# Planning the instruction order of a fused recurrence and MLP anew, with loads modelled as landing later

## The chip, the cores and the metric

The kernel runs on one core of one Trainium2 chip. The metric is the device time of one execution in microseconds (us), the median over several runs. The engines of a core are TensorE (PE in the profile, with its weight loads as PEld), VectorE (DVE), ScalarE (ACT), GpSimd (POOL) and SyncE (SP), which issues the DMA transfers. Each works through its own queue of instructions in order, and waits where an instruction's inputs are not there.

## The reference

A complex diagonal recurrence runs over 768 positions of 32 heads with 48 channels. Its output goes through an MLP with a softplus between two matrices (384 to 2,048 to 384).

```python
def _attn_ref(q, k, v, a_re, a_im):
    B, H, S, D = q.shape                       # 4, 8, 768, 48
    mag = np.sqrt(a_re * a_re + a_im * a_im)
    scale = np.minimum(mag, 0.999) / (mag + 1e-06)
    a_re_n, a_im_n = (a_re * scale, a_im * scale)
    ...
    for t in range(S):
        ar, ai = (a_re_n[:, :, t, :, None], a_im_n[:, :, t, :, None])
        new_re = ar * S_re - ai * S_im
        new_im = ar * S_im + ai * S_re
        kv = np.einsum('bhd,bhe->bhde', k[:, :, t], v[:, :, t])
        S_re, S_im = (new_re + kv, new_im)
        y[:, :, t] = np.einsum('bhd,bhde->bhe', q[:, :, t], S_re)

def _moe_ref(x, w_in, w_out):
    h = x @ w_in                               # 3072 x 384 @ 384 x 2048
    g = np.maximum(h, 0.0) + np.log1p(np.exp(-np.abs(h)))
    return g @ w_out                           # 3072 x 2048 @ 2048 x 384
```

## The kernel before

**Tiles and stages.** The recurrence is cut into chunks of 128 positions. There are 24 chunks: chunk `gc` is position block `gc // 4` of batch `gc % 4`. Four chunks, one block of all batches, make a group of 512 tokens, which is the unit of the MLP. Fourteen slices (0 to 3 with one chunk each, 4 to 13 with two) go through `pre`: ScalarE and VectorE turn `a_re` and `a_im` (the loads of lines 447 and 449, tiles `x_0` to `x_3`, then `x01_4`, `x23_4` and so on) into decays and phases. Line 471 ends the logarithm of the magnitude (tile t1), line 497 sums it along the positions on TensorE for the first four slices (`sum`; a scan at line 480 for the later ones), line 521 is the arctangent, lines 524 to 526 are the sines, and lines 544 and 546 multiply q and k by them. The sines and the arctangent need another ScalarE table than the logarithms and exponentials; line 827 is the place of a table load.

`chunk` then does one chunk. SyncE copies q and k into another layout (`qk`, line 581, ten DMA issues) and loads `v` (line 454). TensorE transposes k (`tr`, line 604), ScalarE copies it (`kt`, lines 609 to 612), TensorE makes the state update (`kv`, line 682), the scores (`sc`, line 627) and the output (`y`, lines 658 and 661); VectorE masks the scores (`a`, line 630). Lines 669 to 671 split y into a high and a low part, `xt0` and `xt1`.

`moe` does the MLP of a group in steps of 128 of the 2,048 hidden channels: nine matmuls for `h` (line 717), three ScalarE passes (lines 722 to 724) and VectorE work (725 to 729) for the softplus and its split into `gh` and `gl`, nine matmuls into the three accumulators `o` (line 741). There are 96 such steps; below, h25 means the 25th h in TensorE's order.

The weights come as eight blocks each of `w_in` and `w_out` (`raw_wi`, `raw_wo`, line 339). They are 64-bit words: VectorE takes their bits apart (349, 352, 355), ScalarE or VectorE rounds (362 or 364), VectorE keeps the rest (366), and `wi0`, `wo0` and so on are ready. Beside this, `inspect` loads all weights once more in 32 pieces (`seen0` to `seen31`, line 384, 384 KB each), and two ScalarE passes (391 and 392) check their size.

**What sets the order.** No queue is written by hand. All of the above are tasks for a `Planner`, each with an engine, a modelled duration, its buffers and a key. `order` plays the program through once, when the kernel is built: at each modelled instant every free engine takes the ready task with the smallest key, and the order in which tasks were taken is the order of the instructions. Keys come from the table `K`: where a slice begins (`head`, `turn`, `tail`), where each chunk, state update, weight block and MLP group stands, how far loads are ahead (`rlead`, `xlead`, `vlead`, `plead`), from where the inspected weights are due (`seen`, and `seenstep` from one to the next), and a few penalties. Some copies and casts may go to ScalarE or VectorE, whichever the model finds free (`alt`). For a DMA the model has one line of transfer: it starts 0.65 us after the issue or when the transfer ahead is done, moves at a fixed rate, and its data are ready a fixed time after. An issue is held back while more than `backlog` us of transfers are outstanding.

When the model finds nothing ready for TensorE, after the first `sum` and before the first `o`, it puts in a filler: one 128x128 matmul whose result nobody reads (line 777), modelled at 0.214 us, so that the array does not stand still. Fillers are ordinary instructions: they are run also if the data are there earlier than modelled.

Of the kernel before, what the change touches and what calls it, by code (L numbers as in the profile page):

```python
# [84 lines left out]
class Planner:  # L85
# [48 lines left out]
    def order(self, filler, until, gate):  # L134
        for t in self.tasks:
            t.left = len(t.deps)
            t.ready = 0.0
            for d in t.deps:
                d.outs.append(t)
        engines = ("PE", "ACT", "DVE", "POOL", "SP")  # L140
        free = dict.fromkeys(engines, 0.0)
        pend = {e: [] for e in engines}
        alts = {"POOL": [], "ACT": [], "DVE": []}
        for t in self.tasks:
            if not t.left:
                pend[t.eng].append(t)
        live, users, queue, slots = {}, {}, {}, {}
        first = {}
        for t in reversed(self.tasks):
            t.key = min([t.key] + [o.key for o in t.outs])  # L150
        for t in self.tasks:
            for b in t.bufs:
                first.setdefault(b, (t.key, t.idx))
        for b in sorted(first, key=lambda b: first[b]):
            queue.setdefault(b.tag, []).append(b)
            live[b.tag] = set()
            slots[b.tag] = list(range(b.bufs))

        def room(t):
            need = {}  # L160
            for b in t.bufs:
                if b not in live[b.tag]:
                    need.setdefault(b.tag, []).append(b)
            for tag, bs in need.items():
                if len(live[tag]) + len(bs) > bs[0].bufs or not all(b in queue[tag][: len(bs)] for b in bs):
                    return False
            return True

        ends, freed = [], []
        dma_free = 0.0  # L170
        table = "log"
        out = []
        now = 0.0
        done = 0
        n = len(self.tasks)
        while done < n:
            for x in [x for x in ends if x[0] <= now]:
                ends.remove(x)
                t = x[1]
                done += 1  # L180
                for b in t.bufs:
                    users[b] = users.get(b, b.users) - 1
                    if users[b] == 0:
                        freed.append((t.end + self.FREE, b))
                for o in t.outs:
                    o.left -= 1
                    o.ready = max(o.ready, t.end + self.LAT[t.eng][o.eng])
                    if not o.left:
                        pend[o.eng].append(o)
                        for a in o.alt:  # L190
                            alts[a].append(o)
            for x in [x for x in freed if x[0] <= now]:
                freed.remove(x)
                live[x[1].tag].discard(x[1])
                slots[x[1].tag].append(x[1].slot)
            nxt = min((x[0] for x in ends + freed), default=None)
            for e in engines:
                if free[e] > now:
                    nxt = free[e] if nxt is None else min(nxt, free[e])
                    continue  # L200
                best = None
                for t in pend[e] + (alts[e] if e in alts else []):
                    if t.ready > now:
                        nxt = t.ready if nxt is None else min(nxt, t.ready)
                        continue
                    if not room(t):
                        continue
                    if e == "SP" and dma_free > now + K["backlog"]:
                        nxt = dma_free - K["backlog"] if nxt is None else min(nxt, dma_free - K["backlog"])
                        continue  # L210
                    if t.eng != e:
                        work = max(0.0, free[t.eng] - now) + sum(
                            u.dur for u in pend[t.eng] if u.ready <= now and (u.key, u.idx) < (t.key, t.idx))
                        if work + t.dur < t.alt[e][0] + K["altpen"]:
                            continue
                    k = t.key + (K["tpen"] if t.tab and t.tab != table else 0.0)
                    if best is None or (k, t.idx) < best[0]:
                        best = ((k, t.idx), t)
                if best is None and e == "PE" and ends and gate.end and not until.end:
                    t = Task("PE", 0.214, filler, 0, -1, None, 0)  # L220
                    free[e] = now + self.array(now, t.dur)
                    t.end = free[e]
                    out.append(t)
                    nxt = min(nxt, free[e]) if nxt is not None else free[e]
                if best is None:
                    continue
                t = best[1]
                pend[t.eng].remove(t)
                if t.eng != e:
                    t.dur, t.fn = t.alt[e]  # L230
                    t.eng = e
                for a in t.alt:
                    if t in alts[a]:
                        alts[a].remove(t)
                for b in t.bufs:
                    if b not in live[b.tag]:
                        live[b.tag].add(b)
                        queue[b.tag].remove(b)
                        b.slot = slots[b.tag].pop(0)
                dur = t.dur  # L240
                if t.tab and t.tab != table:
                    dur += K["table"]
                    table = t.tab
                if e == "PE":
                    dur = self.array(now, dur)
                free[e] = now + dur
                t.end = now + dur
                if e == "SP":
                    dma_free = max(dma_free, now + dur + 0.65) + t.nbytes / 360e3
                    t.end = dma_free + 0.9  # L250
                ends.append((t.end, t))
                out.append(t)
                nxt = min(nxt, free[e]) if nxt is not None else free[e]
            if done < n:
                assert nxt is not None and (nxt > now or any(x[0] <= now for x in ends)), [(e, [(t.key, t.idx, [b.name for b in t.bufs]) for t in pend[e]][:6]) for e in engines]
                now = max(now, nxt)
        self.span = now
        return out
# [18 lines left out]
class Prog:  # L277
# [651 lines left out]
    def tokens(self):  # L929
# [72 lines left out]

K = {
    "head": [
        147.46, 624.17, -734.94, 397.74, -65.21, 161.81, 154.84, 126.74, 332.35, 200.17, 1147.56, 464.07,
        422.42, 1751.28,
    ],
    "turn": [
        875.87, 931.1, 671.81, 372.5, 881.48, 209.67, 360.72, 269.87, 526.4, 568.29, 228.13, 811.71, 706.01,
        1996.71,  # L1010
    ],
    "tail": [
        -334.95, 866.41, -128.28, 1028.77, 17.61, 491.11, 317.86, 1067.36, 517.27, 187.54, 259.83, 490.08,
        795.91, 848.69,
    ],
    "chunk": [
        -267.74, -147.68, 202.11, 211.6, 177.5, 1433.56, 639.03, 1244.43, 174.52, 599.91, 1309.15, 2182.89,
        343.73, 939.25, 322.68, 1047.42, 1525.38, 564.81, 348.78, 1828.49, 378.39, 329.92, 407.62, 379.87,
    ],
    "state": [  # L1020
        -1424.69, -194.39, -93.44, -28.82, 43.46, 43.95, 100.96, 52.68, 129.28, 129.32, 145.62, 150.03,
        185.36, 156.97, 189.71, 254.96, 277.69, 291.22, 297.54, 306.48, 1107.79, 715.4, 146.67, 173.29,
    ],
    "wgt": [
        96.27, -203.72, -101.3, 339.5, -596.58, 402.72, -145.78, 1172.96, 397.64, 873.73, 429.78, 354.94,
        258.65, 1931.67, 500.63, 58.25,
    ],
    "moe": [
        39.42, 84.93, 163.49, 185.18, 356.83, 370.86, 421.4,
    ],  # L1030
    "step": [
        2.126, 3.53, 0.332, 5.405, 0.484, 6.552, 40.863,
    ],
    "seen": 130.1,
    "seenstep": 19.706,
    "rlead": 77.677,
    "xlead": -372.318,
    "vlead": -60.991,
    "plead": -498.518,
    "backlog": 1.925,  # L1040
    "altpen": -0.18,
    "tpen": 9.371,
    "table": 1.3,
}

# [64 lines left out]
```

## Time and profile before

| what | us |
|---|---|
| median of 3 runs | 617.56 |
| lowest and highest of them | 616.93, 620.88 |
| the profiled execution, its own time | 621.91 |
| its span, first to last instruction | 620.2 |
| TensorE busy | 591.4 |
| ScalarE busy | 441.8 |
| VectorE busy | 437.6 |

All rows that are quoted below come from that one profiled execution. A row of the order of time gives start and length in us, engine, line, operation, result and inputs, shapes, the number of instructions merged (x), and in brackets the idle time of the engine just before it with the instruction or DMA that ended it. A row of a group gives busy time and the mean length in ns, then the idle time before its members. Lengths of TensorE rows overlap, since matmuls are pipelined: what a row takes is the distance to the start of the next. ScalarE, VectorE and TensorE are all busy most of the time, so the question at each place is which of them the others wait for.

### The profile page before, as it was taken

The numbers are of one execution on the slowest core, as the hardware profiler recorded it, in microseconds if no ns is written. First come the engines' busy times: TensorE is split into PE (matmuls) and PEld (weight loads), VectorE is DVE, ScalarE is ACT, GpSimd is POOL, SyncE is SP. The second block draws the span as 40 slices with busy tenths as digits, with TensorE's granted clock in tenths as the row PEclk, the third lists the DMA queues.
The fourth block names the chain that finished last, engine by engine and source line by source line (L and its number), as shares of the span: only waits on it lengthen the run. The fifth ranks groups of instructions, "written<-read, shape, count | busy, mean of one in ns | idle before, by whom it ended". The sixth has DMA issues, their size and how long they took to land.

```text
span 620.2 us, 11238 instructions
## 1 busy us (share of the span) xinstructions
PE 591.4 (95%) x4388; PEld 497.0 (80%) x4388; DVE 437.6 (71%) x653; ACT 441.8 (71%) x813; POOL 1.8 (0%) x16
## 2 busy tenths in 40 slices
PE   1999999999999998999999999999999989999995
PEld 1999998787878886878788888888788868888883
DVE  4698989989989886667784559777757624433532
ACT  7958596958997784956974696877949645568652
POOL 1000000000000000000000000000000000000000
PEclk9999999999999997999999999999999989999998
DMA  8948845244004354255340337135324420018002
GB/s 328 382 136 262 308 155 166 59 127 142 26 1 108 128 149 147 66 144 177 99 112 1 130 84 217 43 85 208 82 61 143 112 93 2 1 47 284 1 1 56
DMA packets 50940, 75.53 MB, mean 122 GB/s; under 512 B 5824, under 2 KB 42176, under 8 KB 50880
## 3 DMA queue, kind: packets, MB, share of 16 engines
q1 hardware_dynamic: 50880, 74.73, 38.8%
q8 instruction: 37, 0.61, 0.4%
q14 instruction: 23, 0.19, 0.1%
HBM read 50.33 MB, written 5.51 MB: 90 GB/s over the span
## 4 chain that ended last, share of the span: by engine, by line
PE 60%; ACT 14%; DVE 13%; DMA 7%; SPq 3%; issue 2%; DVEq 0%; ACTq 0%
PE o L741 21%; PE h L717 21%; PE sc L627 5%; PE o L777 4%; PE kv L682 3%; DMA x<-dense_dram 3%; ACT L827 2%; SPq L581 2%; DVE lt L725 2%; DMA seen<-w_out_dram 2%; PE y L661 2%; ACT lt L722 1%; PE y L658 1%; DVE t L480 1%; ACT lt L724 1%
## 5 line engine op out<-in xcount | busy, mean ns | idle before, releaser
L717 PE MATMUL h<-xt,wi 128*128 128x512 f32 x864 | 222.9, 403 | 4.7 <-DVE lt L725 2.5
L741 PE MATMUL o<-gh,wo 128*128 128x512 f32 x576 | 197.7, 400 | 0.4 <-ACT gh L728 0.4
L717 PEld LDWEIGHTS h<-xt,wi 128*128 128x128 f32 x864 | 161.9, 191 | 43.7 <-DVE lt L725 3.9
L725 DVE SCALAR_TENSOR_TENSOR lt<-h,lt 128x512 f32<-128x512 f32 x96 | 65.9, 688 | 104.2 <-ACT lt L724 104.1
L741 PEld LDWEIGHTS o<-gh,wo 128*128 128x128 f32 x576 | 108.4, 188 | 26.8 <-issue 1.6
L722 ACT ACTIVATE lt<-h 128x512 f32<-128x512 f32 x96 | 57.0, 594 | 85.9 <-PE h L717 83.6
L741 PE MATMUL o<-gl,wo 128*128 128x512 f32 x288 | 113.9, 396 | 0.7 <-DVE gl L729 0.7
L724 ACT ACTIVATE lt<-lt,one 128x512 f32<-128x512 f32 x96 | 69.5, 724 | 2.1
L729 DVE TENSOR_TENSOR gl<-lt,gh 128x512 fp32r<-128x512 f32 x96 | 66.0, 688 | 6.8 <-ACT gh L728 5.2
L741 PEld LDWEIGHTS o<-gl,wo 128*128 128x128 f32 x288 | 54.3, 188 | 13.6 <-DVE gl L729 2.1
L723 ACT ACTIVATE lt<-lt 128x512 f32<-128x512 f32 x96 | 60.6, 631 | 2.1
L627 PE MATMUL sc<-qk 96*128 96x128 f32 x384 | 49.7, 283 | 0.0
L627 PEld LDWEIGHTS sc<-qk 96*128 96x128 f32 x384 | 47.7, 198 | 1.5 <-issue 0.2
L777 PE MATMUL o<-ident 128*128 128x128 f32 x378 | 46.8, 279 | 0.0
L777 PEld LDWEIGHTS o<-ident 128*128 128x128 f32 x378 | 44.7, 195 | 0.6 <-issue 0.6
L480 DVE TENSOR_TENSOR_SCAN t<-hold,t 128x384 f32<-128x384 bf16 x40 | 36.1, 945 | 4.2 <-DMA out_dram<-o 3.3
L827 ACT ACT_TABLE_LOAD x28 | 35.9, 1283 | 0.5
L544 DVE TENSOR_TENSOR x<-x,t 128x1536 f32<-128x1536 f32 (+1 forms) x14 | 21.4, 1527 | 19.1 <-ACT t L526 19.1
L630 DVE TENSOR_TENSOR a<-sc,mask 128x512 f32<-128x512 f32 x48 | 32.3, 683 | 3.2 <-PE sc L627 3.2
L682 PEld LDWEIGHTS kv<-v,kt 128*96 128x96 f32 x320 | 29.8, 166 | 5.1 <-ACT kt L609 3.7
L391 ACT ACTIVATE seen<-seen 128x384 f32<-128x384 f32 x32 | 17.4, 547 | 22.2 <-DMA seen<-w_out_dram 18.0
L682 PE MATMUL kv<-v,kt 128*96 128x64 f32 (+1 forms) x320 | 29.9, 247 | 2.8 <-ACT kt L609 2.8
(90 smaller groups left out, 629.0 us busy)
## 6 DMA issues: line engine op xcount, KB each, us to landing
x<-dense_dram SPq DMA_DIRECT2D x20, 768.0 KB, 5.8
qk<-x SPq DMA_DIRECT2D x96, 144.0 KB, 3.3
raw_wi<-w_in_dram SPq DMA_DIRECT2D x8, 768.0 KB, 10.5
raw_wo<-w_out_dram SPq DMA_DIRECT2D x8, 768.0 KB, 10.1
seen<-w_in_dram SPq DMA_DIRECT2D x16, 384.0 KB, 3.8
seen<-w_out_dram SPq DMA_DIRECT2D x16, 384.0 KB, 3.9
v<-vpad_dram SPq DMA_DIRECT2D x24, 224.0 KB, 2.7
out_dram<-o SPq DMA_DIRECT2D x18, 256.0 KB, 3.2
```

What stands on the lines that cost most here:

```text
L480: V.tensor_tensor_scan(out()[:, s], self.hold, inc()[:, s], 0.0, ALU.mult, ALU.add)
L627: PE.matmul(psc()[:, hh * P : (hh + 1) * P], q[:, h, CH:], q[:, h, :CH], start=True, stop=True)
L682: PE.matmul(kv()[: 2 * D, s], k[:, h, :, :].rearrange("p c d -> p (c d)"), v[:, s], start=h == 0, stop=h == H - 1)
L717: PE.matmul(h()[:, :n], w()[:, q, i, fs], x()[:, i, :n], start=k == 0, stop=k == 3 * NI - 1)
L722: add("ACT", a1(n) - 0.04, lambda: A.activation(tv(), h(), AF.Abs), k, r=[h], w=[t])
L723: add("ACT", a1(n), lambda: A.activation(tv(), tv(), AF.Exp, scale=-1.0), k, w=[t], tab="log")
L724: add("ACT", a1(n, 1), lambda: A.activation(tv(), tv(), AF.Ln, bias=self.one), k, w=[t], tab="log")
L725: add("DVE", d1(n), lambda: V.scalar_tensor_tensor(tv(), h(), 0.0, tv(), ALU.max, ALU.add), k, r=[h], w=[t])
L729: add("DVE", d1(n), lambda: V.tensor_tensor(gl(), tv(), gh().bitcast(F32), ALU.subtract), k, r=[t, gh], w=[gl])
L741: PE.matmul(acc[m]()[:, :n], w()[:, wq, f % 2, ms], x(), start=f == f0 and q == 0, stop=f == f1 - 1 and q == 2)
L777: self.nc.tensor.matmul(self.acc0[0]()[:, :P], self.ident, x, start=True, stop=True)
L827: nc.scalar.preload_act_table_set(TABLES[table])
```

## The change

The model of a DMA gets a lower rate (330 GB/s for 360) and a later landing (2.0 us after the transfer for 0.9). Nothing else in the code differs but the table `K`, all of whose keys are other numbers; a few rows of it are shown.

```diff
                 if e == "SP":
-                    dma_free = max(dma_free, now + dur + 0.65) + t.nbytes / 360e3
-                    t.end = dma_free + 0.9
+                    dma_free = max(dma_free, now + dur + 0.65) + t.nbytes / 330e3
+                    t.end = dma_free + 2.0
...
     "wgt": [
-        96.27, -203.72, -101.3, 339.5, -596.58, 402.72, -145.78, 1172.96, 397.64, 873.73, 429.78, 354.94,
-        258.65, 1931.67, 500.63, 58.25,
+        447.27, -1169.33, -352.53, 1086.75, -1104.67, 201.72, -638.13, 1996.3, 1081.53, 701.56, 725.41,
+        1796.95, 1182.85, 1292.24, 1033.56, 59.41,
     ],
...
-    "seen": 130.1,
-    "seenstep": 19.706,
...
-    "backlog": 1.925,
...
+    "seen": 222.447,
+    "seenstep": 23.851,
...
+    "backlog": 3.992,
```

The work is the same, task for task; what moves is the order, which engine does some of the copies and casts, and the number of fillers. Before, 182 fillers stand ahead of the first h and 7 behind it; now 155 and 1. Three places follow, as the instruction queues have them (the number behind a tile's name tells buffers apart).

TensorE, from the second half of chunk 3's scores to the first h, before:

```order
L627 MATMUL sc3_1_747<-qk3_631 128x128 x4
L777 MATMUL o0_153<-ident_58 128x128 x12
L661 MATMUL y3_774<-a3_0_762,v3_546 32x128 x6
L661 MATMUL y3_774<-a3_1_767,v3_546 32x128 x6
L661 MATMUL y3_774<-a3_0_762,v3_546 32x128 x2
L661 MATMUL y3_774<-a3_1_767,v3_546 32x128 x2
L777 MATMUL o0_153<-ident_58 128x128 x32
L717 MATMUL h_849<-xt0_0_434,wi0_838 128x512
```

and now:

```order
L627 MATMUL sc3_1_730<-qk3_594 128x128 x4
L777 MATMUL o0_162<-ident_58 128x128 x20
L661 MATMUL y3_773<-a3_0_752,v3_556 32x128 x6
L661 MATMUL y3_773<-a3_1_762,v3_556 32x128 x6
L661 MATMUL y3_773<-a3_0_752,v3_556 32x128 x2
L661 MATMUL y3_773<-a3_1_762,v3_556 32x128 x2
L777 MATMUL o0_162<-ident_58 128x128 x16
L717 MATMUL h_822<-xt0_0_470,wi0_809 128x512
```

The 32 fillers behind y3 became 16, and the 12 ahead of it 20.

VectorE in the first twenty microseconds, from the end of slice 0's logarithm (t_0, line 471) on, before:

```order
L471 SCALAR_TENSOR_TENSOR t_0_104<-t_0_104,x_0_97 128x384
L471 SCALAR_TENSOR_TENSOR t_1_114<-t_1_114,x_1_100 128x384
L504 COPY car00_157<-sum0_0_144 128x3
L460 TENSOR_TENSOR x_3_106<-x_3_106,t_3_148 128x384
L461 TENSOR_TENSOR t_3_148<-x_3_106,t_3_148 128x384
L462 SCALAR_TENSOR_TENSOR t_3_148<-t_3_148,x_3_106 128x384
L504 COPY car00_157<-sum0_1_164 128x3
L534 TENSOR_SCALAR t_0_104<-sum1_0_178 128x384
```

and now:

```order
L471 SCALAR_TENSOR_TENSOR t_0_108<-t_0_108,x_0_97 128x384
L349 TENSOR_SCALAR bits_wo0_146<-raw_wo0_106 128x768
L352 SCALAR_TENSOR_TENSOR bits_wo0_146<-raw_wo0_106,bits_wo0_146 128x768
L460 TENSOR_TENSOR x_3_103<-x_3_103,t_3_133 128x384
L471 SCALAR_TENSOR_TENSOR t_1_113<-t_1_113,x_1_99 128x384
L461 TENSOR_TENSOR t_3_133<-x_3_103,t_3_133 128x384
L355 SCALAR_TENSOR_TENSOR bits_wo0_146<-raw_wo0_106,bits_wo0_146 128x768
L462 SCALAR_TENSOR_TENSOR t_3_133<-t_3_133,x_3_103 128x384
L364 CAST wo0_178<-bits_wo0_146 128x768
L349 TENSOR_SCALAR bits_wi2_185<-raw_wi2_111 128x768
L366 TENSOR_TENSOR wo0_178<-bits_wo0_146,wo0_178 128x768
L534 TENSOR_SCALAR t_0_108<-sum1_0_180 128x384
```

The conversion of wo0, and the start of wi2's, now stand between the steps of slices 1 and 3; before, the first conversion came after line 544 of slices 0 and 1. SyncE's queue has `raw_wo0` as the sixth load now and as the ninth before. Its first four are the first halves of x_0 to x_3 now; before, x_0's second half stood second.

ScalarE around the copies of chunk 11's transposed k (kt11), before:

```order
L724 ACTIVATE lt_2423<-lt_2423,one_66 128x512
L391 ACTIVATE seen2_2385<-seen2_2385 128x384
L670 ACTIVATE xt0_2_2231<-y10_2389 128x3x128
L609 ACTIVATE kt11_2450<-tr11_0_2430 128x6x48
L611 ACTIVATE kt11_2450<-tr11_0_2430 128x2x32
L612 ACTIVATE kt11_2450<-tr11_0_2430 128x2x16
```

and now:

```order
L722 ACTIVATE lt_2203<-h_2181 128x512
L609 ACTIVATE kt11_2215<-tr11_0_2198 128x6x48
L611 ACTIVATE kt11_2215<-tr11_0_2198 128x2x32
L612 ACTIVATE kt11_2215<-tr11_0_2198 128x2x16
L723 ACTIVATE lt_2203<-lt_2203 128x512
```

The inspection of seen2 is gone from there. In the whole queue of ScalarE, `seen0` to `seen19` stood between h10 and h71 before, with seen17 to seen19 just ahead of the last softplus steps before the last xt copy; now seen0 stands at h31, seen1 to seen6 one or two at a time from h39 to h61, seen7 to seen19 from h66 to h73, and the last two xt copies come at about h80. The last twelve stood at h85 to h88 and now stand at h82 to h86. SyncE issues the loads of seen8 to seen19 in one row, ahead of chunk 22's qk copies. Chunk 21's `v` is now loaded right after chunk 12's and holds one of two buffers until it is used, and of each pair of chunks from 4 to 11 the second now comes first.

More of the change, by code (lines that the diff above doesn't have):

```diff
@@ L1004 @@
     "head": [
-        147.46, 624.17, -734.94, 397.74, -65.21, 161.81, 154.84, 126.74, 332.35, 200.17, 1147.56, 464.07,
-        422.42, 1751.28,
+        279.77, -427.35, -608.06, 1112.01, -382.0, 2092.52, 1109.0, 125.77, 1480.94, 212.31, 3501.1,
+        1428.05, 993.45, 2973.25,
     ],
     "turn": [
-        875.87, 931.1, 671.81, 372.5, 881.48, 209.67, 360.72, 269.87, 526.4, 568.29, 228.13, 811.71, 706.01,
-        1996.71,
+        838.1, 2182.21, 26.83, 2545.51, 543.36, 1011.04, 1086.57, 1100.59, 194.11, 1313.48, 1205.39, 952.86,
@@ L1011 @@
+        1682.66, 633.89,
     ],
     "tail": [
-        -334.95, 866.41, -128.28, 1028.77, 17.61, 491.11, 317.86, 1067.36, 517.27, 187.54, 259.83, 490.08,
-        795.91, 848.69,
+        -1181.59, 1452.08, -696.88, 1047.03, 16.44, 880.0, 140.45, 208.97, 165.06, 204.82, 435.6, 1030.94,
+        629.47, 927.47,
     ],
     "chunk": [
-        -267.74, -147.68, 202.11, 211.6, 177.5, 1433.56, 639.03, 1244.43, 174.52, 599.91, 1309.15, 2182.89,
-        343.73, 939.25, 322.68, 1047.42, 1525.38, 564.81, 348.78, 1828.49, 378.39, 329.92, 407.62, 379.87,
+        -305.7, -127.85, -52.02, 1186.11, 850.99, 937.04, 451.81, 1162.03, 1645.12, 1197.97, 3836.66,
@@ L1019 @@
+        3705.09, 884.03, 1582.02, 1817.55, 867.03, 2483.85, 480.6, 468.06, 2776.45, 737.43, 335.83, 1601.75,
+        866.21,
     ],
     "state": [
-        -1424.69, -194.39, -93.44, -28.82, 43.46, 43.95, 100.96, 52.68, 129.28, 129.32, 145.62, 150.03,
-        185.36, 156.97, 189.71, 254.96, 277.69, 291.22, 297.54, 306.48, 1107.79, 715.4, 146.67, 173.29,
+        -1075.67, -562.16, -74.15, -55.04, 42.17, 42.15, 124.28, 52.66, 127.87, 127.81, 170.28, 136.28,
+        177.98, 214.35, 263.57, 269.92, 282.32, 283.58, 307.92, 308.11, -54.9, 560.48, -30.85, 1099.72,
@@ L1023 @@
     ],
     "wgt": [
-        96.27, -203.72, -101.3, 339.5, -596.58, 402.72, -145.78, 1172.96, 397.64, 873.73, 429.78, 354.94,
-        258.65, 1931.67, 500.63, 58.25,
+        447.27, -1169.33, -352.53, 1086.75, -1104.67, 201.72, -638.13, 1996.3, 1081.53, 701.56, 725.41,
+        1796.95, 1182.85, 1292.24, 1033.56, 59.41,
     ],
     "moe": [
-        39.42, 84.93, 163.49, 185.18, 356.83, 370.86, 421.4,
+        39.42, 85.41, 191.39, 199.16, 308.86, 604.45, 651.11,
     ],
     "step": [
-        2.126, 3.53, 0.332, 5.405, 0.484, 6.552, 40.863,
+        2.124, 3.514, 0.368, 5.555, 2.48, 3.085, 52.481,
@@ L1033 @@
     ],
-    "seen": 130.1,
-    "seenstep": 19.706,
[L1036 to L1039, printed above, removed]
-    "backlog": 1.925,
-    "altpen": -0.18,
-    "tpen": 9.371,
+    "seen": 222.447,
+    "seenstep": 23.851,
+    "rlead": -841.096,
+    "xlead": -596.339,
+    "vlead": 133.79,
+    "plead": -38.02,
+    "backlog": 3.992,
+    "altpen": -0.173,
+    "tpen": 24.534,
     "table": 1.3,
```

## The prediction, made before the change was run

> **What bounds the kernel now.** I read the page first, then TensorE's rows in order of time with their idle gaps, then ScalarE's and VectorE's rows at the places where TensorE stood still. The page's span and the busy time of each engine, with its share and its instructions:
>
> ```profile
> span 620.2 us, 11238 instructions
> PE 591.4 (95%) x4388; PEld 497.0 (80%) x4388; DVE 437.6 (71%) x653; ACT 441.8 (71%) x813; POOL 1.8 (0%) x16
> ```
>
> TensorE bounds it: 95% busy. But it is not busy with work all the time. Its rows in the first stretch (start, length, then operation; a record is one weight load's matmul pass, so each program matmul of 128x128 appears as two) show what it does until the first MoE matmul:
>
> ```profile
> 12.76 1.62 PE L497 MATMUL sum<-mask,t 128*128 128x128 f32 x6 [12.76 <-DVE t L471]
> ...
> 19.12 9.10 PE L777 MATMUL o<-ident 128*128 128x128 f32 x80
> 28.05 1.50 PE L497 MATMUL sum<-mask,t 128*128 128x128 f32 x12
> ...
> 74.34 7.41 PE L777 MATMUL o<-ident 128*128 128x128 f32 x64
> 81.51 4.45 PE L717 MATMUL h<-xt,wi 128*128 128x512 f32 x18
> ```
>
> Line 777 is the filler, work without a result that the planner puts in where it expects TensorE to have nothing. From 12.76 to 81.51 us no idle is shown: fillers cover all waiting, so the head's length on TensorE is its real work plus its fillers. Forty fillers (80 records) take 28.05 - 19.12 = 8.93 us, 0.223 us each.
>
> After 81.51 TensorE runs almost without a gap. The gaps that cost most, with an undisturbed run of the same three operations (kv, sc, h) ahead of them:
>
> ```profile
> 224.05 1.48 PE L682 MATMUL kv<-v,kt 128*96 128x64 f32 x16
> 225.37 2.02 PE L627 MATMUL sc<-qk 96*128 96x128 f32 x16
> 227.14 2.34 PE L717 MATMUL h<-xt,wi 128*128 128x512 f32 x9
> 229.41 1.08 PE L658 MATMUL y<-qk,s 96*32 96x128 f32 x32
> ...
> 239.16 1.79 PE L682 MATMUL kv<-v,kt 128*96 128x64 f32 x16 [2.78 <-ACT kt L609]
> 240.75 3.75 PE L627 MATMUL sc<-qk 96*128 96x128 f32 x16
> 244.15 3.70 PE L717 MATMUL h<-xt,wi 128*128 128x512 f32 x9
> 247.78 1.08 PE L658 MATMUL y<-qk,s 96*32 96x128 f32 x32
> ...
> 441.82 2.36 PE L717 MATMUL h<-xt,wi 128*128 128x512 f32 x9 [1.51 <-DVE lt L725]
> ...
> 505.03 0.49 PE L717 MATMUL h<-xt,wi 128*128 128x512 f32 x1 [1.31 <-ACT xt L670]
> 506.31 5.77 PE L717 MATMUL h<-xt,wi 128*128 128x512 f32 x17 [0.78 <-DVE xt L671]
> 511.91 0.39 PE L741 MATMUL o<-gh,wo 128*128 128x512 f32 x1
> ...
> 514.00 2.26 PE L717 MATMUL h<-xt,wi 128*128 128x512 f32 x9
> 516.10 0.39 PE L741 MATMUL o<-gh,wo 128*128 128x512 f32 x1
> ```
>
> The wait at 239 costs more than its 2.78 us: kv, sc and h then take 247.78 - 239.16 = 8.62 us where they took 229.41 - 224.05 = 5.36, so 3.26 more, 6.04 in all. The pair at 505 costs 1.31 + 0.78 = 2.09, and its 17 matmuls take 511.91 - 506.31 = 5.60 us where nine take 2.10 (516.10 - 514.00), so 17 take 3.97: 1.63 more, 3.7 in all. What ScalarE did just before each, and the wait totals of the inspected weights:
>
> ```profile
> 235.76 0.55 ACT L391 ACTIVATE seen<-seen 128x384 f32<-128x384 f32 x1 [4.21 <-DMA seen<-w_in_dram]
> ...
> 497.84 0.56 ACT L391 ACTIVATE seen<-seen 128x384 f32<-128x384 f32 x1 [6.10 <-DMA seen<-w_out_dram]
> ...
> ACT seen L391: 22.2, 9
> ...
> DMA to landing us min/median/max: 3.0/3.9/6.3
> ```
>
> Both times ScalarE stood at line 391 until a `seen` load landed, 4.21 and 6.10 us, and the copies of kt and xt that TensorE needs stood behind it in its queue.
>
> **The change part by part.** *Head.* The order of the changed kernel has 155 fillers ahead of the first h, that of before 182. If nothing else is late, the head gets 27 x 0.223 = 6.0 us shorter. Is the cover real, or will TensorE now wait instead? The last filler run of before ends at 81.51 because of VectorE, which finishes wi0 there; its two rows, and VectorE by stretches (columns: length, then busy time of PE, PEld, DVE, ACT, POOL, clock, DMA share, GB/s):
>
> ```profile
> 77.04 0.55 DVE L349 TENSOR_SCALAR bits_wi<-raw_wi 128x768 int32<-128x768 int32 x1
> ...
> 80.21 0.96 DVE L366 TENSOR_TENSOR wi<-bits_wi,wi 128x768 fp32r<-128x768 f32 x1
> ...
> 0.00:20.00 20.00, 7.25 (x40) 7.28 (x41) 9.65 (x21) 15.54 (x35) 1.76 (x16) 1.00 0.92 347
> 20.00:40.00 20.00, 20.00 (x185) 20.00 (x184) 15.71 (x25) 14.27 (x28) 0.00 (x0) 1.00 0.73 248
> 40.00:60.00 20.00, 20.00 (x235) 19.36 (x234) 19.19 (x30) 15.30 (x37) 0.00 (x0) 1.00 0.72 243
> 60.00:81.50 21.50, 21.50 (x239) 20.86 (x239) 19.58 (x28) 14.75 (x21) 0.00 (x0) 1.00 0.88 311
> ```
>
> VectorE is full from 40 to 81 and idle for 14.6 of the first 40 us. The change moves the conversions of wo0, wi2 and wi3 into that idle time. It also gives VectorE three casts (line 364) and one xt copy (669) that ScalarE had, and takes one state copy from it: three more in all, at about the 0.55 us of the row above, against 14.6 us of idle. So the head can really shrink; I take the filler count, 6.0. Bounds: -7, if TensorE also starts a microsecond earlier (x_1's first half, ahead of which one load of 384 KB less now goes, 1.1 us at the 347 GB/s of the first stretch); -3, if half comes back as waits on the early conversions. Their load is the risk: VectorE reaches wo0 right after line 471 of t_0, which in before let TensorE start at 12.76. There wo0's load was issued at 4.58 and took 10.1 us, so it landed at 14.7:
>
> ```profile
> 4.58 0.45 SPq L339 DMA_DIRECT2D raw_wo<-w_out_dram  x1
> ...
> DMA to landing us min/median/max: 10.1/10.1/10.1
> ```
>
> It now goes ahead of v0, x_2's second half and wi2, 1,376 KB (1.41 MB), which take 4.1 us at those 347 GB/s: it lands near 10.6, two us early.
>
> *Fillers after the first h.* Seven before, one now: 6 x 0.223 = 1.3 us off.
>
> *Inspected weights.* Before, `seen0` to `seen19` lie scattered from h10 to h71 on ScalarE, one ahead of kt11 (the wait at 239), three ahead of the last xt copy (the wait at 505). Now the first is at h31, seven are scattered up to h61, thirteen stand together from h66 to h73, and none lies between h74 and the last two xt copies near h80, nor near kt11. Both waits lose their cause: 6.0 + 3.7 = 9.7 us off. What is late next at these places is the h itself, whose inputs ScalarE then has ready. Bounds: 0, if the same waits form elsewhere; -11.2, if the wait at 441 goes too. I take 9.7 and keep the 1.5 at 441, since the x load ahead of it is still there.
>
> On the planner's new landing time: issue 0.45 + 0.65 + 384 KB (0.393 MB) at 330 GB/s (1.19) + 2.0 gives 4.3 us for a `seen` load, the old one 3.1. The measured median, 3.9, lies between, nearer the new. [...]
>
> *The rest* (fewer casts on ScalarE, chunk 5 ahead of chunk 4, v21 loaded early) I cost at nothing: after 81.5 TensorE is covered by its own queue of h and o.
>
> Sum, against the profiled execution: 621.9 (span 620.2 and 1.7 around it) - 6.0 - 1.3 - 9.7 = 604.9. The profiled execution is 4.3 us above the median of 617.6, perhaps by larger waits of just this kind; so I do not subtract that again and predict 605.
>
> **The rivals.** *Waits move.* The head gains, but ScalarE still meets late loads at other places: 621.9 - 7.3 = 614.6, or 610.3 from the median. For it: nine waits averaged 2.5 us, and the new landing time is only 1.2 us later. Against: the two that cost were at two places now empty.
>
> *TensorE cold in the head.* With 27 fillers fewer, data that are late leave TensorE idle, and after it slow: the 6.0 are not gained and 3.3 more are lost, as after the wait at 239; 621.9 - 1.3 - 9.7 + 3.3 = 614.2. Against: wo0's two us of margin. [...]
>
> *Slower.* The thirteen `seen` together, h67 to h73: one takes ScalarE 1.2 us (562.49 - 561.28 in the rows below), thirteen 15.6, beside seven times the three passes of the softplus (0.59 + 0.63 + 0.72 = 1.95, 13.6) and two table loads for slice 13 (2.6), 31.8 us, while TensorE needs 14 x 2.1 = 29.4 for its h and o. If each also waits for its load as the nine did (2.5), 32 us more stand on ScalarE ahead of h: 605 + 2.4 + 32 = 639. It ends slower than before once the waits pass (17.0 - 2.4) / 13 = 1.1 us each. Against: before has such a row of them, and there one waited, and TensorE did not:
>
> ```profile
> L722 ACT ACTIVATE lt<-h 128x512 f32<-128x512 f32 x96 | 57.0, 594 | 85.9 <-PE h L717 83.6
> ...
> L724 ACT ACTIVATE lt<-lt,one 128x512 f32<-128x512 f32 x96 | 69.5, 724 | 2.1
> ...
> L723 ACT ACTIVATE lt<-lt 128x512 f32<-128x512 f32 x96 | 60.6, 631 | 2.1
> ...
> L827 ACT ACT_TABLE_LOAD x28 | 35.9, 1283 | 0.5
> ...
> 561.28 0.55 ACT L391 ACTIVATE seen<-seen 128x384 f32<-128x384 f32 x1 [2.15 <-DMA seen<-w_out_dram]
> 562.49 0.53 ACT L391 ACTIVATE seen<-seen 128x384 f32<-128x384 f32 x1
> ...
> 560.00:580.00 20.00, 20.00 (x87) 16.20 (x86) 6.55 (x11) 18.59 (x45) 0.00 (x0) 1.00 0.59 202
> ```
>
> **How the numbers follow.** Forecast 0.56; all waits gone and the median's distance kept (599 and below) 0.07; waits move 0.20; cold head 0.10; slower 0.07. About 1% is what a measurement of this kernel can tell from no change: below 611.4 is faster, above 623.7 slower. Faster: 0.56 + 0.07 + half of the moved waits 0.10 + half of the cold head 0.05 = 0.78; the same 0.15; slower 0.07. The range goes from 599 (617.6 - 17.0 - 1.5) to 613 (617.6 - 3 - 1.3) and leaves out about 0.2.
>
> **What would show it.** Right: first h near 75.5, with no idle on TensorE from 13 us on; no gap behind a kt or xt copy near h25 and h81; line 391's waits well under 22 us. Wrong: idle ahead of sums or tr in the head; VectorE waiting at line 349 for wo0; idle ahead of h67 to h73; half-speed stretches at new places.

## The result and the profile after

| | before | after |
|---|---|---|
| median of 4 runs each, us | 618.70 | 609.24 |
| lowest and highest, us | 616.93, 620.88 | 607.64, 611.35 |
| profiled execution, us | 621.91 | 611.35 |
| its span, us | 620.2 | 609.6 |
| first h, us | 81.51 | 80.66 |
| first h to the end of the span, us | 538.7 | 528.9 |

The ratio of the times is 0.9847, with a 95% interval from 0.980 to 0.9895: faster by about 1.5%. Ratios, here and below, leave out one slow run: 636.68 us with the new table alone, at a lower granted clock (0.977) than all others. The last two rows of the table tell where the 10.6 us between the two profiled executions went: 9.8 us behind the first h, and only 0.85 us ahead of it. From the page of the kernel after, the span and the busy time of the engines:

```profile
span 609.6 us, 11134 instructions
...
PE 582.6 (96%) x4322; PEld 489.8 (80%) x4322; DVE 442.4 (73%) x664; ACT 434.8 (71%) x802; POOL 1.8 (0%) x16
```

The 27 fillers are gone from the head, and yet the first h comes at nearly the old time. TensorE's rows in the head, in order of time (start, length, operation, and in brackets the idle time ahead and what ended it):

```profile
51.52 1.72 PE L682 MATMUL kv<-v,kt 128*96 128x64 f32 x16 [1.53 <-DMA v<-vpad_dram]
53.05 1.51 PE L604 MATMUL tr<-ident,x 128*128 128x128 f32 x6
54.34 5.03 PE L777 MATMUL o<-ident 128*128 128x128 f32 x36
59.21 1.48 PE L682 MATMUL kv<-v,kt 128*96 128x64 f32 x16
...
67.59 0.46 PE L627 MATMUL sc<-qk 96*128 96x128 f32 x2 [1.12 <-issue]
68.20 1.95 PE L627 MATMUL sc<-qk 96*128 96x128 f32 x14 [0.15 <-DMA qk<-x]
69.94 6.18 PE L777 MATMUL o<-ident 128*128 128x128 f32 x40
76.05 1.08 PE L661 MATMUL y<-a,v 128*32 128x128 f32 x32
...
80.66 4.44 PE L717 MATMUL h<-xt,wi 128*128 128x512 f32 x18
```

TensorE stands still twice, 1.53 us for chunk 2's `v` and 1.12 + 0.15 us for chunk 3's `qk`. After each it is slow for a while: the 40 filler records take 76.05 - 69.94 = 6.11 us, and 4.56 in a run where nothing was late (below). The trace shows why: the granted clock stands at 0.50 from 52.70 to 56.11 and from 69.77 to 73.18 us (last section). The profile counts these slow stretches as busy time (PE 3.41 of 3.41 us in both). The chain of waits of the same execution, and SyncE's rows, name the transfers:

```profile
42.08 9.31 DMA v<-vpad_dram
...
61.25 6.90 DMA qk<-x
```

```profile
36.60 0.45 SPq L447 DMA_DIRECT2D x<-dense_dram  x1
...
40.48 0.53 SPq L339 DMA_DIRECT2D raw_wo<-w_out_dram  x1
41.05 0.93 SPq L339 DMA_DIRECT2D raw_wi<-w_in_dram  x1
42.08 0.38 SPq L454 DMA_DIRECT2D v<-vpad_dram  x1
```

`v2` is 224 KB and took 9.31 us to land, behind wo7 and wi4, two loads of 768 KB that were still under way when it was issued: they landed at 45.8 and 50.7 us, `v2` at 51.4. (x01_4, issued at 36.60, had landed by 41.6.) In the kernel before, wi4 went at 17.59 and v2 at 42.94 ahead of x01_4 and wo7. The longest of SyncE's own waits from 38 to 66 us, after (engine and line, what it waited for, us, times, longest):

```profile
SPq L581 <- DMA raw_wi<-w_in_dram: 3.3, 1, 3.3
```

A `qk` issue of chunk 2, which has nothing to do with wi4, stood 3.3 us until wi4 had landed. The program shows why: in it the transfers of this queue signal eight semaphores in turn, and an issue waits for the eighth transfer ahead of it. Three rows of SyncE's queue in the kernel after, with their number and the semaphores that each waits for:

```
33 L581 DMA qk1_360<-x_1_99 16x256 [waits DMAHW0_49]
...
41 L339 DMA raw_wi4_465<-w_in_dram 128x1536 [waits DMAHW0_49]
...
49 L581 DMA qk2_481<-x_2_101 48x3x256 [waits DMAHW0_49,DVE_49]
```

So the large loads delayed twice here: `v2`, behind wo7 and wi4 in the line (9.31 us to landing), and the eighth issue behind wi4 (3.3 us). The late `qk` of chunk 3 follows from the first: the chain runs from `v2` by way of chunk 2's state update and ScalarE's copies to its issues, the last of which go behind another load of 768 KB, x01_5.

Behind the first h, the gaps at 239 and 505 us are gone, and line 391 waits 9.0 us in all where it waited 22.2. In their place stand these, from TensorE's order of time and the answer on the tile `seen`:

```profile
139.62 0.49 PE L717 MATMUL h<-xt,wi 128*128 128x512 f32 x1 [1.46 <-ACT xt L670]
140.30 5.77 PE L717 MATMUL h<-xt,wi 128*128 128x512 f32 x17 [0.18 <-DVE xt L671]
145.90 1.48 PE L682 MATMUL kv<-v,kt 128*96 128x64 f32 x16
...
493.00 2.36 PE L717 MATMUL h<-xt,wi 128*128 128x512 f32 x9 [1.27 <-DVE lt L725]
```

```profile
  ACT seen L391: 9.0, 5
```

The one near 140 is new: chunk 6's copies `xt0` and `xt1` stand behind the work on wi4. It costs 1.64 us of idle and 145.90 - 140.30 = 5.60 us for 17 matmuls that take 3.97 at full speed, 3.3 us together. The one at 493 is the row of thirteen `seen`, with two table loads among them, which costs 1.27 us and not the tens of the slower rival.

### The profile page after: what moved, and what is told of

It reads as the page before. It is cut to its first block, busy times and chain, and to the rows that moved or that the text cites. A ratio compares the mean times of both kernels' runs of the same rounds, so it can differ in the third digit from the quotient of the medians.

```text
span 609.6 us, 11134 instructions
## 1 busy us (share of the span) xinstructions
PE 582.6 (96%) x4322; PEld 489.8 (80%) x4322; DVE 442.4 (73%) x664; ACT 434.8 (71%) x802; POOL 1.8 (0%) x16
## 4 chain that ended last, share of the span: by engine, by line
PE 67%; DVE 12%; ACT 9%; DMA 5%; SPq 3%; issue 3%; DVEq 0%
PE h L717 25%; PE o L741 24%; PE sc L627 5%; PE kv L682 3%; PE o L777 3%; SPq L581 3%; PE y L658 2%; PE y L661 2%; DMA v<-vpad_dram 2%; DMA qk<-x 1%; DMA x<-dense_dram 1%; DVE lt L725 1%; PE tr L604 1%; ACT L827 1%; DMA seen<-w_out_dram 1%
## 5 line engine op out<-in xcount | busy, mean ns | idle before, releaser
L627 PEld LDWEIGHTS sc<-qk 96*128 96x128 f32 x384 | 46.2, 192 | 3.8 <-issue 1.6
L777 PE MATMUL o<-ident 128*128 128x128 f32 x312 | 40.4, 289 | 0.0
L777 PEld LDWEIGHTS o<-ident 128*128 128x128 f32 x312 | 39.2, 206 | 0.4 <-issue 0.4
L728 ACT ACTIVATE gh<-lt 128x512 fp32r<-128x512 f32 x35 | 22.1, 630 | 14.5 <-DVE lt L725 14.4
```

The lines of the kernel that those rows point to most:

```text
L627: PE.matmul(psc()[:, hh * P : (hh + 1) * P], q[:, h, CH:], q[:, h, :CH], start=True, stop=True)
L777: self.nc.tensor.matmul(self.acc0[0]()[:, :P], self.ident, x, start=True, stop=True)
```

## The experiments

All move tasks in the list that the planner gives back, by two helpers put ahead of `class Prog` (so line numbers are 16 to 21 higher in these kernels than in the two shown; where only the table or the model is exchanged they are the same). `reorder` wraps the planner's list in `fast`; each experiment is its body. The kernel before ran beside each group, at medians of 617.9 to 618.4 us.

```python
def pick(seq, eng, *names):   # tasks of one engine that touch all the named tiles
    return [t for t in seq if t.eng == eng and all(any(b.name == n for b in t.bufs) for n in names)]

def behind(seq, moved, anchor):
    rest = [t for t in seq if t not in moved]
    i = max(rest.index(t) for t in anchor) + 1
    return rest[:i] + moved + rest[i:]
```

**Loads moved back.** On the kernel after, wo7 and wi4 go behind chunk 3's `qk`:

```diff
+    late = pick(seq, "SP", "raw_wo7") + pick(seq, "SP", "raw_wi4")
+    seq = behind(seq, late, pick(seq, "SP", "qk3"))
```

> The changed kernel, with the loads raw_wo7 and raw_wi4 (768 KB each) issued behind chunk 3's qk copies instead of just ahead of v2; nothing else differs. Theory A (the transfers ahead of v2 in the line delay it: it took 9.3 us to land): v2 lands in about 9.3 - 3.8 = 5.5 us, kv2 does not wait any more (1.53 us before), TensorE stays at full speed behind it, the first h comes at about 76 to 77 us instead of 80.66, and the time falls by 4 to 5 us, ratio to the kernel before about 0.978. Theory B (SyncE's own pace of 0.66 us for each qk copy sets the end of the head): kv2 runs earlier but the first h moves by less than 1 us, and the time stays within 1 us of the changed kernel's, ratio 0.984.

Measured: 605.83 us (5 runs), ratio 0.9801 (0.9779 to 0.9824). TensorE's rows:

```profile
49.74 1.48 PE L698 MATMUL kv<-v,kt 128*96 128x64 f32 x16
...
55.75 1.48 PE L698 MATMUL kv<-v,kt 128*96 128x64 f32 x16
...
64.82 4.63 PE L793 MATMUL o<-ident 128*128 128x128 f32 x40
69.38 1.08 PE L677 MATMUL y<-a,v 128*32 128x128 f32 x32
...
73.98 4.43 PE L733 MATMUL h<-xt,wi 128*128 128x512 f32 x18
...
101.74 1.16 PE L643 MATMUL sc<-qk 96*128 96x128 f32 x8 [1.26 <-DVE a L646]
```

No gap is shown from 12 to 97 us, and the first h stands at 73.98, 7.5 us ahead of before: that is the head which the filler count promised. Against the kernel after it is 6.7 us in the two profiles, but 2.9 to 3.4 us in the medians, where 4 to 5 had been expected. One reason is that the head of the kernel after is not late by the same in every execution: two experiments below leave it as it is, and have their first h at 77.32 and 78.27, with 1.98 and 2.39 us of idle ahead of it, and 4.56 and 5.46 us for the 40 filler records behind (6.11 in the first profile). Another is that a part comes back at 101.74, where VectorE waited for `x01_6`. Its issue came late; SyncE's waits from 72 to 110 us:

```profile
SPq L597 <- DMA raw_wo<-w_out_dram: 3.3, 1, 3.3
```

The `qk` of chunk 5 stood there for wo6, the eighth transfer ahead.

**The copies, three times.** On the kernel after, first only ScalarE's order changes, wi4's cast behind `xt0`:

```diff
+    cast = pick(seq, "ACT", "bits_wi4", "wi4")
+    rest = pick(seq, "DVE", "bits_wi4", "wi4")
+    copy = pick(seq, "ACT", "y6", "xt0_1") + pick(seq, "DVE", "y6", "xt1_1")
+    seq = behind(seq, cast + rest, copy)
```

> The changed kernel, with ScalarE's cast of wi4 put behind the copy of chunk 6's xt0 instead of ahead of it. Theory: the wait at 139 us (1.46 + 0.18 us) and the half-speed stretch behind it (17 matmuls in 5.6 us instead of 4.0) come from that cast waiting for VectorE; both go, 3.3 us off, ratio about 0.979. Rival: something else is late there (VectorE's own part of the split, which stands behind the conversion of wi5), a gap of about 1 us stays, and less than 1 us is gained, ratio 0.984.

Measured: 608.79 us (6 runs), ratio 0.9848 (0.9812 to 0.9884), no change against the kernel after. `xt0` came earlier, and TensorE waited 1.85 us for `xt1` instead, as the rival had it:

```profile
136.96 5.78 PE L735 MATMUL h<-xt,wi 128*128 128x512 f32 x17 [1.85 <-DVE xt L689]
```

The same edit with the loads moved back as well:

> The changed kernel with both edits, the two loads behind chunk 3's qk copies and the cast of wi4 behind chunk 6's xt0. If both causes are right and independent, the gains add: 609.2 - 4.5 - 3.3 = 601.4 us, ratio 0.972. If what is gained in the head is given back in the stretch behind it (VectorE is full there), the ratio is that of the cast alone, about 0.979.

Measured: 607.51 us (6 runs), 0.9819 (0.9793 to 0.9845). The gains did not add to the 601.4 of the first reading: the loads moved alone gave 605.83, and the two intervals overlap, so this edit is worth nothing clear with the loads moved either. Then both copies were put ahead, VectorE's too:

```diff
+    cast = pick(seq, "ACT", "bits_wi4", "wi4")
+    seq = behind(seq, cast, pick(seq, "ACT", "y6", "xt0_1"))
+    copy = pick(seq, "DVE", "y6", "xt1_1")
+    words = [t for t in pick(seq, "DVE", "bits_wi5") if seq.index(t) < seq.index(copy[0])]
+    seq = behind(seq, words, copy)
```

> The kernel after, with chunk 6's two copies (xt0 on ScalarE, xt1 on VectorE) taken ahead of the work on wi4 and wi5 that stood in front of them; loads unchanged. Theory (VectorE's word operations and ScalarE's cast of wi4 hold the first h of chunk 6): the wait near 137 to 140 us falls from 1.64 us to under 0.7 us and the 17 h matmuls behind it take about 4.0 us instead of 5.77, so 1 to 2.8 us less than the kernel after, 606.5 to 608.3 us. Rival (the wait only goes to the next user, wi4's or wi5's first h): no change, 609 us. In the head nothing is touched: v2 is late or not, as in the kernel after (first h 77 to 81).

Measured: 609.56 us (4 runs), ratio 0.9841 (0.9802 to 0.988). The rival held:

```profile
136.45 4.21 PE L736 MATMUL h<-xt,wi 128*128 128x512 f32 x17 [0.39 <-DVE xt L690]
...
143.80 3.05 PE L736 MATMUL h<-xt,wi 128*128 128x512 f32 x9 [1.81 <-DVE lt L744]
```

The wait fell to 0.39 us as expected, and 1.81 us came back seven us later at the first softplus. VectorE is full here, 14.93 of 15.00 us in this run (columns: length, then busy time of PE, PEld, DVE, ACT, POOL, clock, DMA share, GB/s):

```profile
131.00:146.00 15.00, 12.36 (x123) 10.03 (x123) 14.93 (x23) 9.02 (x20) 0.00 (x0) 0.97 0.48 174
```

So in these orders VectorE's work was late somewhere in this stretch, and the order chose who waited for it. That no order could avoid the wait is not shown.

**Copies and loads, with the loads only a little back.** wo7 and wi4 behind `v3`, and both copies ahead:

```diff
+    late = pick(seq, "SP", "raw_wo7") + pick(seq, "SP", "raw_wi4")
+    seq = behind(seq, late, pick(seq, "SP", "v3"))
```

> The same copies, and the loads of wo7 and wi4 put behind the load of v3 (not behind qk3 as in the run with only the loads moved). Theory: v2 lands in time, first h at 74 to 76 us; if qk3 meets the moved loads it is up to 1 us late. With the copies 1 to 2.8 us less than the 605.8 of the moved loads alone: 603 to 605 us. Rival (the moved loads hold chunk 4's or chunk 5's x instead, as 1.26 us near 101 us did with the loads moved): 605.5 to 607 us.

Measured: 609.35 us (6 runs), ratio 0.9859 (0.983 to 0.9889): worse than expected by 4 us. `v2` was in time, but the loads now met the next two small transfers, TensorE's rows with 0.69 and 1.93 us of idle:

```profile
58.67 1.80 PE L648 MATMUL sc<-qk 96*128 96x128 f32 x14 [0.69 <-DMA qk<-x]
...
66.31 2.14 PE L648 MATMUL sc<-qk 96*128 96x128 f32 x16 [1.93 <-issue]
```

**Loads early.** wi4 and wi5 behind wo3, where few bytes are moved, and wo7 behind `qk3`:

```diff
+    early = pick(seq, "SP", "raw_wi4") + pick(seq, "SP", "raw_wi5")
+    seq = behind(seq, early, pick(seq, "SP", "raw_wo3"))
+    seq = behind(seq, pick(seq, "SP", "raw_wo7"), pick(seq, "SP", "qk3"))
```

> The kernel after with the loads of wi4 and wi5 put behind the load of wo3 (their tiles are free from the start, and little is moved between 17 and 36 us), and wo7 behind qk3. Theory (large loads that stand ahead of a small one in the same line make it late): nothing large is ahead of v2 and qk3, first h at 74 us; and the crowd of loads from 59 us on is 1.5 MB smaller than with the loads moved back, so chunk 4's qk and the next x are not held and the 1.26 us near 101 us go too: 602 to 604.5 us, below both kernels and below the 605.8 of the loads moved back. Rival (the head's data are late for another reason, or the early loads hold x and qk0): first h at 77 us or later, 607 us or more.

Measured: 609.94 us (6 runs), ratio 0.9863 (0.9833 to 0.9893). The rival held; SyncE's waits from 17 to 45 us, and TensorE's row:

```profile
SPq L598 <- DMA raw_wi<-w_in_dram: 4.7, 2, 3.2
```

```profile
46.81 3.95 PE L644 MATMUL sc<-qk 96*128 96x128 f32 x16 [3.09 <-issue]
50.55 2.77 PE L794 MATMUL o<-ident 128*128 128x128 f32 x12
```

These loads are out of v2's way and hold chunks 0 and 1 instead: issues of `qk` stand 4.7 us behind them, chunk 1's scores start 3.09 us late, and the first h is again at 80.58.

**The inspected weights alone.** On the kernel before, only `seen2` and `seen17` to `seen19` move out of the way of `kt11` and of the last `xt`:

```diff
+    seq = behind(seq, pick(seq, "ACT", "seen2"), pick(seq, "ACT", "kt11"))
+    late = [t for j in (17, 18, 19) for t in pick(seq, "ACT", f"seen{j}")]
+    seq = behind(seq, late, pick(seq, "DVE", "y22", "xt1_5"))
```

> The kernel before, with the two inspections that stood in the way put later on ScalarE: seen2 behind the copies of kt11, and seen17 to seen19 behind chunk 22's xt0 copy; nothing else differs. Theory (these waits on loads cost TensorE 6.0 and 3.7 us in the middle): both gaps and their half-speed stretches go, 9 to 10 us off, about 609 us, ratio 0.984 to 0.985, as much as the whole change. Rival (waits move): the later place meets a late load as well, or other operations are late at the same places; less than 4 us off, ratio above 0.993.

Measured: 611.38 us (4 runs), ratio 0.9886 (0.9862 to 0.9911), 6.5 us from four moved inspections, where 9 to 10 had been expected. The gaps at 239 and 505 were gone, and the rest behind the first h took 611.8 - 82.28 = 529.5 us, as after.

**Each half of the change alone.** First the new table with loads modelled as before, then the later landing with the old table:

```diff
-                    dma_free = max(dma_free, now + dur + 0.65) + t.nbytes / 330e3
-                    t.end = dma_free + 2.0
+                    dma_free = max(dma_free, now + dur + 0.65) + t.nbytes / 360e3
+                    t.end = dma_free + 0.9
```

> The new table alone; a load is modelled as before (360e3 and 0.9). The order then has 162 fillers ahead of the first h (155 after, 182 before), wi4 and wi5 loaded with the first weights, v2 ahead of wo7, and the inspected weights read late as in the kernel after. Theory (the gain of the middle is the table's reading order; the head's gain was lost to wi4 and wo7 ahead of v2): v2 in time, first h at 75 to 77 us, the rest 529 to 530 us: 605.5 to 608 us. Rival (the later landing is what makes the plan good): data late again in the head and in the middle, 609 us or more.

Measured: 630.56 us (4 runs, from 623.86 to 636.68), ratio 1.0154 (1.0093 to 1.0214), slower than before. The rival held, by more than it said. TensorE's rows, and the waits for inspected weights:

```profile
65.87 2.77 PE L682 MATMUL kv<-v,kt 128*96 128x64 f32 x16 [3.00 <-DMA v<-vpad_dram]
...
505.79 3.91 PE L717 MATMUL h<-xt,wi 128*128 128x512 f32 x9 [3.66 <-DVE lt L725]
```

```profile
  ACT seen L391: 4.8, 5
```

In the head it is the same fault at another chunk: `v3` was issued at 56.01 behind wo7, wo4, wi6 and wo5, and the first h came at 83.13. The rest takes 628.2 - 83.13 = 545.1 us, 16 more than after, with a dozen gaps of 0.6 to 3.7 us, most of them in front of h, though the inspected weights are waited for less than in any other run (4.8 us). At 505 the slower rival's mechanism is seen at work: two table loads of 1.28 us and inspections stand among the softplus passes on ScalarE. The second half alone:

> The later landing alone with the old table: 203 fillers ahead of the first h (182 before) and the inspected weights read as early as before. Theory: 21 fillers more at 0.223 us put the first h at 86 us, and the waits of ScalarE for inspected weights stay: 620 to 624 us. Rival (modelling loads later takes waits away by itself): 612 to 617 us.

Measured: 628.37 us (4 runs), ratio 1.0182 (1.0146 to 1.0218), above both readings. The first h came at 85.25, about as the fillers have it, and the rest took 540.2 us, about as before. That the waits stay was wrong: line 391's fell to 7.9 us. Nothing was won by it: other gaps stand at other places, the longest of them 1.74 us at 263; what causes each was not followed up. Either half makes the kernel slower by 1.5 to 1.8%, both together faster by 1.5%. This table and this model of the loads work as a pair.

**The two kernels once more.** The kernel after:

> The kernel after, unchanged, beside the last one. Theory: 607 to 611 us; its head varies from one execution to the next, since v2 and qk3 are late by more or less (first h between 77 and 81 us). Rival (the 80.66 us of the first profile is what the order fixes): first h again at 80.5 to 81.

Measured: 608.76 us (5 runs), ratio 0.9848 (0.9815 to 0.988). First h at 80.83, where the rival had it, and behind it 609.7 - 80.83 = 528.9 us again. Still the order does not fix the 80.8. TensorE waited 0.68 us for `v2` here and 1.53 in the first profile, for chunk 3's `qk` 1.97 + 0.17 us and 1.12 + 0.15. Idle and half speed add up to the same in these two executions (2.8 us, and 6.83 at half the clock), and to less in the two runs above that have the same head. The kernel before:

> The kernel before, unchanged, profiled once more. Theory: the waits behind ScalarE near 239 and 505 us stand again, 2 to 3 us each, but how long TensorE is slow behind them differs; the rest behind the first h takes 534 to 539 us (538.7 in the first profile, with 4.9 us of half speed in it). Rival (half speed follows from the gap alone): the same 538 to 539 us.

Measured: 618.45 us, span 616.7, first h at 80.94, behind it 535.8 us against 538.7. TensorE's rows:

```profile
238.37 1.92 PE L682 MATMUL kv<-v,kt 128*96 128x64 f32 x14 [2.62 <-ACT kt L609]
...
247.01 1.08 PE L658 MATMUL y<-qk,s 96*32 96x128 f32 x32
...
503.23 0.49 PE L717 MATMUL h<-xt,wi 128*128 128x512 f32 x1 [0.55 <-ACT xt L670]
504.51 4.21 PE L717 MATMUL h<-xt,wi 128*128 128x512 f32 x17 [0.79 <-DVE xt L671]
```

The wait near 239 costs the same 6 us again (2.62, and 247.01 - 238.37 = 8.64 instead of 5.36). The one near 505 costs 1.34 us and hardly any slow stretch, where it cost 3.7.

**Loads spread.** wo7 and wi4 behind `qk3`, and wo5, wi7 and wo6, which are needed last, behind `v7`:

```diff
+    late = pick(seq, "SP", "raw_wo7") + pick(seq, "SP", "raw_wi4")
+    seq = behind(seq, late, pick(seq, "SP", "qk3"))
+    late = [t for n in ("raw_wo5", "raw_wi7", "raw_wo6") for t in pick(seq, "SP", n)]
+    seq = behind(seq, late, pick(seq, "SP", "v7"))
```

> The loads of wo7 and wi4 behind qk3 as in the run with the loads moved, and besides wo5, wi7 and wo6 (converted after 150 us) put behind v7, where SP stands idle from 95 to 107 us. Theory (an issue on SP waits until the eighth one before it has landed, so large loads hold the small ones issued after them): first h at 74 us as there; SP's wait of 3.3 us for wo6's load ahead of qk5 and qk4 goes, x01_6 is issued near 90 us instead of 93.1, VectorE's wait of 2.09 us for it and TensorE's 1.26 us near 101 us go: 1.3 to 2.5 us under the 605.8 of the loads moved alone, 603.3 to 604.5 us. Rival (VectorE's work, not the loads, sets that stretch): 605.5 to 606 us; or the three loads hold v6 or qk7: 606 us or more.

Measured: 604.56 us (6 runs), ratio 0.9781 (0.975 to 0.9813), the lowest median here, and each of its runs (603.65 to 606.12) is below all runs of both kernels; against the run with the loads moved alone (605.83) the intervals overlap. The rows show what was expected: from 30 us on SyncE no longer waits for a weight load, `x01_6` is issued at 89.99 us where it was 93.10, and the gap of 1.26 us near 101 is down to 0.18:

```profile
89.99 0.46 SPq L465 DMA_DIRECT2D x<-dense_dram  x1
```

```profile
74.71 4.42 PE L735 MATMUL h<-xt,wi 128*128 128x512 f32 x18
...
97.94 1.16 PE L645 MATMUL sc<-qk 96*128 96x128 f32 x8 [0.18 <-DVE s L709]
...
133.64 0.50 PE L735 MATMUL h<-xt,wi 128*128 128x512 f32 x1 [1.46 <-ACT xt L688]
```

## Why the prediction was right, and where it was off

Faster was right, and the time lies in the range; the forecast of 605.0 was 4.2 us below the median of 609.24. Of the signs that it names, two for right came (no gap behind the kt and xt copies, line 391's waits at 9.0 us), one did not (first h near 75.5), and one for wrong came (half-speed stretches at new places). The sum took 17.0 us off the profiled execution; 10.6 went between the profiled executions, 9.5 between the medians. That the number still came this near is in part luck: the head of the kernel after is slow to a different degree in each execution (first h from 77.32 to 80.83 with the same order), a thing that the prediction did not reckon with. By its steps:

- **Head, 6.0 us: it failed.** It measured 0.85 in the first pair of profiles and 0.1 in the second (80.94 to 80.83). The filler count itself was right: with nothing late the head ends at 73.98 or 74.71, even beyond the 75.5 foretold, 0.8 us of which is TensorE's earlier start (11.97 for 12.76), as the bound of -7 had it. What failed is "if nothing else is late". The step watched wo0's load, and rightly found it in time; but the change also moves wi4 and wo7 into the queue ahead of v2 and qk3, and these were not followed. The lost 6.7 us (80.66 - 73.98) are 2.8 us of idle (1.53 + 1.12 + 0.15) and 3.3 us of slow rows behind it: of these, 76.05 - 68.20 = 7.85 us where 6.21 are full speed, 1.6, and 59.21 - 51.52 = 7.69 where 6.01 are, 1.7. Some 0.6 us are not traced to rows.
- **The cold-head rival, given 0.10,** is what happened in the head, by other loads than the one weighed against it, and milder: it had the 6.0 lost and 3.3 more, and in the profiles the idle and the slow rows about used up the 6.0 and no more. Its 614.2 holds the gain of the middle and starts from the profiled execution; the profiled execution after took 611.35.
- **Fillers behind the first h and inspected weights, 1.3 + 9.7 = 11.0 us: right in cause, somewhat large in size.** Behind the first h 9.8 us went in the first pair of profiles and 6.9 in the second (535.8 to 528.9); moving four inspections alone gave 6.5 us in the medians. The 9.7 were read from one execution, in which the gap at 505 was followed by a slow stretch that the second one lacks. The prediction noticed that this execution was 4.3 us above the median, "perhaps by larger waits of just this kind", and this is borne out in part: the two waits cost 9.7 us in it, and about 6 and 1.34 in the second profile, 3.5 us faster.
- **The rest, put at nothing: a wait was taken over there.** The reason given was that behind 81.5 TensorE is covered by its own queue of h and o. Near 140 it is not: 3.3 us (1.7 where no slow stretch follows, as in the second profile) stand against the saving. VectorE is busy there nearly without a gap (14.90 of the 15.00 us from 131 on), and in the experiments on the copies the wait moved and did not go.
- **The row of thirteen `seen`:** 1.27 us, as the forecast had it; the slower rival fell for the kernel after, and showed its mechanism with the new table alone.

## What to carry over

Where a change moves large loads, list for each small transfer that the critical engine needs which large ones now stand ahead of it in its queue, and, where completion semaphores are used in turn as in this program, which of them the next issues must wait for; the fillers removed here were worth their time with that list clear (first h at 73.98 us) and not without (80.66). Take the price of a wait from more than one execution, its slow stretch apart from its idle. Here the table of order and the model that it was made with had to be changed together.

## What the runs showed of the hardware

**A slow stretch was there or not, and had one of two sizes.** Asked by stretches, the trace gives the clock granted to TensorE. In the first profiles of the two kernels it stands at 1.00 or 0.50 wherever it is recorded. But for the last ten microseconds it is 0.50 from 240.32 to 247.15 and from 506.56 to 509.98 us before, and from 52.70 to 56.11, 69.77 to 73.18 and 141.45 to 144.86 us after: once for 6.83 us and four times for 3.41. At half speed that loses 3.4 and 1.7 us; the rows behind the waits lost 3.26 and 1.63 us before, and 1.7, 1.6 and 1.63 after. Below is the wait for chunk 3's `qk` in the second profile of the kernel after and in the run with only ScalarE's copy moved, whose heads have the same order, and the wait for `v2` in the first profile (columns as above: after the length, PE's busy time; the clock is third from the end):

```profile
63.41:66.82 3.41, 1.27 (x31) 0.84 (x23) 2.09 (x2) 1.22 (x2) 0.00 (x0) 1.00 1.03 278
66.82:73.65 6.83, 6.83 (x32) 6.83 (x33) 5.79 (x9) 3.00 (x6) 0.00 (x0) 0.50 1.00 411
```

```profile
62.50:65.91 3.41, 1.53 (x37) 1.14 (x35) 2.83 (x3) 0.48 (x1) 0.00 (x0) 1.00 1.01 321
65.91:69.32 3.41, 3.29 (x27) 3.13 (x28) 1.67 (x3) 1.67 (x4) 0.00 (x0) 1.00 0.90 348
```

```profile
49.29:52.70 3.41, 1.88 (x21) 1.72 (x20) 3.07 (x5) 1.94 (x5) 0.00 (x0) 1.00 0.96 242
52.70:56.11 3.41, 3.41 (x20) 3.41 (x19) 0.96 (x1) 2.83 (x7) 0.00 (x0) 0.50 0.63 179
```

The 40 filler records behind the first of these waits take 76.22 - 69.85 = 6.37 us, behind the second 4.56. In the first profile of the kernel after the two stretches of the head begin at 52.70 and 69.77 us, 17.07 apart or five times 3.41; in that of the kernel before the two begin 266.24 us apart, 78 times 3.413.

The length of a wait alone did not tell what came behind it. Idle of 1.53 us and of 1.12 + 0.15 us in the first profile of the kernel after had 3.41 us of half speed behind it, and 1.97 + 0.17 us in the second had 6.83. Idle of 1.98 us in the run with only ScalarE's copy moved had none (clock 1.00 from 66 to 73 us), nor had 1.51 us at 441.82 in the first profile of the kernel before (1.00 from 440 to 447); behind 2.02 us at 440.75 in its second profile, nine h took 2.36 us, the same as behind the 1.51. What decides stays open.

**A small load landed late behind large ones.** 224 KB of `v` took 9.31 us behind two loads of 768 KB still under way, and `v` loads took 2.5 to 5.5 us in the kernel before from 36 to 80 us.
